# Block transposes on VectorE and four-row-tile scores in a fused attention and MLP kernel

## The chip, the cores and the metric

The kernel runs on one core of a Trainium2 chip. Its metric is device microseconds of the whole program. A profiled execution gives, beside its time, the span from the first to the last instruction and a record of every instruction; the engines are TensorE (PE for matmuls, PEld for the weight loads ahead of them), VectorE (DVE), ScalarE (ACT), GpSimd (POOL, which here mostly issues DMAs) and SyncE (SP, which issues the stores).

## The reference

Sigmoid attention over 8 batches, 12 heads, 448 positions and 64 columns a head; its result, with heads put side by side, is the input of a two-layer MLP with a gated sigmoid.

```
q, k, v: (8, 12, 448, 64)        w_in: (768, 2048)   w_out: (2048, 768)   beta: (2048,)

scores = q @ k.T / sqrt(64) - log(448)
attn   = sigmoid(scores) @ v                          # (8, 12, 448, 64)
x      = attn.transpose(0, 2, 1, 3).reshape(3584, 768)
h      = x @ w_in
out    = (h * sigmoid(beta * h)) @ w_out              # (3584, 768), float32
```

Inputs are float32; the kernel casts them to float16 as they are loaded, accumulates in float32 and stores float32.

## The kernel before

**Units.** A slot is a pair of heads of one batch: six slots a batch, 48 in all. A duo is two slots, four heads. `load_duo` (L82) fetches q, k and v of four heads with DMAs from the POOL queue: partition p of 112 takes the four consecutive positions 4p to 4p+3, 256 values of each head. So column tile s4 of a head holds the positions 4p+s4, and the keys' four tiles and the queries' columns stay in that order through the whole kernel; the stores at the end undo it.

**From raw to scores.** `put_in_order` (L120) copies one slot's q and k on VectorE so that the two heads' 64 columns lie side by side for each s4. `transposes` (L129) turns that into eight transposes on TensorE (128 columns by 112 rows each, written to the PSUM tile `qkT_ps`), and one VectorE copy brings them to `qkT`: rows 0 to 63 are the first head, 64 to 127 the second, columns are positions. `scores` (L141) multiplies a tile of 112 keys with up to 448 queries, contracting 64 rows; the two heads of the slot lie on the two halves of the rows. The result `sco` is two PSUM banks, and one ACT instruction (L162) makes its sigmoid into `attnT`. There are two `sco` tiles. `attend` (L172) multiplies with v: eight matmuls, the two heads on the two halves of the output's partitions, into a PSUM tile of its own (`ps_av`), and a VectorE cast (L188) puts it into the batch's `xT`.

**The dense part.** `dense1` (L194) makes one 128-row piece of h from `xT` (six matmuls, L200), its sigmoid on ACT (L208) and the product on VectorE (L211) into `gt`. `dense2` (L215) makes half of a 128-row output tile (sixteen matmuls, L219), copied by VectorE (L229) into `osb`; after the second half the tile is stored from SP, in up to two pieces that put the rows back to their positions. `dense1`, `dense2` and `transposes` share three PSUM buffers (`ps_one`).

**Order.** Everything is issued in an order written out by hand; each engine runs its own instructions in that order.

- Start: loads of three duos and the first weights; eleven idle matmuls to keep TensorE running; `put_in_order` and `transposes` for the first slots.
- First loop: the six slots of batch 0, queries 0 to 223, each with `attend` of the slot before. Further weights and duos are fetched in between.
- Second loop: the same slots with queries 224 to 447, with eleven dense units filled in; `load_w_out` is fetched here.
- Main loop: steps h = 12 to 95, two to a slot. A step computes two key tiles of a slot's scores (L152, four matmuls), then as many dense units from a list (`filler_stream`) as a time budget allows. At a slot's first step `attend` of the slot before comes first and `put_in_order(s + 2)` is queued; at its second step `transposes(s + 2)` follows the scores. Every second slot the duo three ahead is loaded. The raw tiles have three buffers, the v tiles five.
- End: the last `attend` and the remaining dense units.

Of the kernel before, what the change touches and what calls it, by code (L numbers as in the profile page):

```python
# [14 lines left out]
def kernel(  # L15
# [10 lines left out]

    nc = tc.nc
# [6 lines left out]
    P = 128  # L41
    S4 = 4
    SP = S // S4
    NPAIR = H // 2
    NHC = DM // P
# [7 lines left out]
    NSLOT = B * NPAIR  # L53

# [3 lines left out]
    qkp = ctx.enter_context(tc.tile_pool(name="qkp", bufs=2))  # L58
    qkTp = ctx.enter_context(tc.tile_pool(name="qkTp", bufs=8))
    attnp = ctx.enter_context(tc.tile_pool(name="attnp", bufs=8))  # L60
# [5 lines left out]
    ps_av = ctx.enter_context(tc.tile_pool(name="ps_av", bufs=1, space=bass.MemoryType.PSUM))  # L66
    ps_one = ctx.enter_context(tc.tile_pool(name="ps_one", bufs=3, space=bass.MemoryType.PSUM))

    ident = const.tile([P, P], FP16, name="ident")
# [8 lines left out]

# [3 lines left out]
    def load_duo(d: int, what="qkv", slots=(0, 1)):  # L82
        b, tp = divmod(2 * d, NPAIR)
        if d not in raws:
            raws[d] = rawp.tile([SP, 2, 4, S4 * D], FP16, tag="raw", name="raw")
            vs[d] = vp.tile([SP, 4, S4 * D], FP16, tag="v16", name="v16")
        h0, h1 = 2 * slots[0], 2 * slots[-1] + 2
        for nm, dst, srct in (("q", raws[d][:, 0], q), ("k", raws[d][:, 1], k), ("v", vs[d], v)):
            if nm in what:
                nc.gpsimd.dma_start(  # L90
                    out=dst[:, h0:h1, :],
                    in_=srct[b, 2 * tp + h0 : 2 * tp + h1].rearrange(
                        "h (p s4) d -> p h (s4 d)", s4=S4
                    ),
                )

# [16 lines left out]

# [4 lines left out]
    qks = {}  # L118

    def put_in_order(s: int):  # L120
        d, i = divmod(s, 2)
        qk = qkp.tile([SP, 2, S4, 2, D], FP16, tag="qk", name="qk16")
        nc.vector.tensor_copy(  # L123
            out=qk.rearrange("p r s4 h d -> p r h s4 d"),
            in_=raws[d][:, :, 2 * i : 2 * i + 2, :].rearrange("p r h (s4 d) -> p r h s4 d", s4=S4),
        )
        qks[s] = qk

    def transposes(s: int):  # L129
        qk = qks.pop(s)  # L130
        ps = ps_one.tile([P, 2, S], FP16, tag="one", name="qkT_ps")
        for reg in range(2):
            for s4 in range(S4):
                nc.tensor.transpose(  # L134
                    ps[:, reg, s4 * SP : (s4 + 1) * SP], qk[:, reg, s4], ident[0:SP, 0:SP]
                )
        t = qkTp.tile([P, 2, S], FP16, tag="qkT", name="qkT")
        nc.vector.tensor_copy(out=t, in_=ps)  # L138
        qkT[s] = t

    def scores(s: int, c0: int, n: int, jts):  # L141

        t = qkT[s]
        per = S // n
        todo = []
        for i in range(0, len(jts), per):
            js = jts[i : i + per]
            sco = ps_sc.tile([SP, 2, 512], FP32, tag="sco", name="sco")
            for u, jt in enumerate(js):
                for hh in range(2):  # L150
                    lo, hi = hh * D, (hh + 1) * D
                    nc.tensor.matmul(  # L152
                        sco[:, hh, u * n : (u + 1) * n],
                        t[lo:hi, 1, jt * SP : (jt + 1) * SP],
                        t[lo:hi, 0, c0 : c0 + n],
                        start=True,
                        stop=True,
                    )
            todo.append((js, sco))
        for js, sco in todo:  # L160
            at = attnp.tile([SP, 2, S], FP16, tag="attnT", name="attnT")
            nc.scalar.activation(  # L162
                out=at,
                in_=sco[:, :, 0:S],
                func=AF.Sigmoid,
                bias=nlogs[0:SP, 0:1],
                scale=MSCALE,
            )
            for u, jt in enumerate(js):
                at_tiles[s, jt, c0] = at[:, :, u * n : (u + 1) * n]  # L170

    def attend(s: int, c0: int, n: int):  # L172
        b, tp = divmod(s, NPAIR)
        d, i = divmod(s, 2)
        if b not in xTs:
            xTs[b] = xTp.tile([P, NHC, S], FP16, tag="xT", name="xT")
        av = ps_av.tile([P, 512], FP32, tag="av", name="av_ps")
        for jt in range(S4):
            at = at_tiles.pop((s, jt, c0))
            for hh in range(2):  # L180
                nc.tensor.matmul(  # L181
                    av[hh * D : (hh + 1) * D, 0:n],
                    vs[d][:, 2 * i + hh, jt * D : (jt + 1) * D],
                    at[:, hh],
                    start=(jt == 0),
                    stop=(jt == S4 - 1),
                )
        nc.vector.tensor_copy(out=xTs[b][:, tp, c0 : c0 + n], in_=av[:, 0:n])  # L188

# [25 lines left out]
    def dense2(w: int, t: int, half: int):  # L215
        gt = gts[w]
        m2 = ps_one.tile([P, HALF], FP32, tag="one", name="m2_ps")
        for dc in range(NDC):
            nc.tensor.matmul(  # L219
                m2,  # L220
                gt[:, dc, t * P : (t + 1) * P],
                w_out16[:, dc, half * HALF : (half + 1) * HALF],
                start=(dc == 0),
                stop=(dc == NDC - 1),
            )
        if half == 0:
            osbs[w, t] = outp.tile([P, DM], FP32, tag="osb", name="osb")
        osb = osbs[w, t]
        nc.vector.tensor_copy(out=osb[:, half * HALF : (half + 1) * HALF], in_=m2)  # L229
        if half == 1:  # L230
            c, end = t * P, (t + 1) * P
            while c < end:
                b, s4, p0 = 2 * w + c // S, (c % S) // SP, c % SP
                n = min(end - c, SP - p0)
                rows = out[b * S : (b + 1) * S].rearrange("(p s4) dm -> s4 p dm", s4=S4)
                r0 = c - t * P
                nc.sync.dma_start(out=rows[s4, p0 : p0 + n], in_=osb[r0 : r0 + n, :])
                c += n
            osbs.pop((w, t))
# [6 lines left out]
    def filler_stream():  # L246

        for c0 in (0, QH):
            for dc in range(NDC):
                yield M1H_US, 0, lambda dc=dc, c0=c0: dense1(0, dc, c0, QH)  # L250
        for b in range(B):
            if b > 0:
                for dc in range(NDC):
                    yield M1_US, 2 * NPAIR * (b + 1), lambda b=b, dc=dc: dense1(b, dc)
            for t in tiles_after(b):
                for half in range(2):
                    yield M2_US, 0, lambda b=b, t=t, half=half: dense2(b // 2, t, half)
# [9 lines left out]

    with tc.manual_schedule():
        load_duo(0, "qk", (0,))
        make_identity(nc, ident)  # L270
# [10 lines left out]
        load_duo(0, "qk", (1,))  # L281
        load_duo(0, "v")
        load_duo(1)
        load_duo(2)
        load_w_in(0)
        load_w_in(1)
        put_in_order(0)
        transposes(0)
        put_in_order(1)
        transposes(1)  # L290
        put_in_order(2)


        for s in range(NPAIR):
            scores(s, 0, QH, range(S4))
            if s >= 1:
                attend(s - 1, 0, QH)
            if s + 2 < NPAIR:
                transposes(s + 2)
            if s + 3 < NPAIR:  # L300
                put_in_order(s + 3)
            if s == 0:
                load_w_in(2)
            if s == 1:
                load_duo(3)
            if s == 2:
                load_w_in(3)
            if s == 4:
                load_duo(4)

        for s in range(NPAIR):
            scores(s, QH, QH, range(S4))
# [7 lines left out]
            if s == 4:  # L320
                put_in_order(6)
            if s == 5:
                put_in_order(7)
                transposes(6)
# [7 lines left out]
        for h in range(2 * NPAIR, 2 * NSLOT):  # L332
            s, g = divmod(h, 2)
            if g == 0:
                if s == NPAIR:
                    attend(s - 1, QH, QH)
                else:
                    attend(s - 1, 0, S)
                if s > NPAIR and s + 2 < NSLOT:
                    put_in_order(s + 2)  # L340
                if s % 2 == 0:
                    d = s // 2 + 2 if s == NPAIR else s // 2 + 3
                    while d <= s // 2 + 3 and d < NSLOT // 2:
                        load_duo(d)
                        d += 1
            scores(s, 0, S, (2 * g, 2 * g + 1))
            if s == NPAIR and g == 0:
                transposes(s + 1)
                put_in_order(s + 2)
            if g == 1 and s + 2 < NSLOT:  # L350
                transposes(s + 2)
            i = h - 2 * NPAIR
            budget += first / 7 if i < 7 else second / 5 if i < 12 else rest
            while at_fill[0] < len(fill):
# [4 lines left out]
                fill_units(1)  # L359
        attend(NSLOT - 1, 0, S)  # L360
# [31 lines left out]
```

## Time and profile before

| | us |
|---|---|
| median of three runs (lowest, highest) | 441.91 (441.15, 443.85) |
| span of the profiled execution | 439.7 |
| PE busy | 423.2 |
| ACT busy | 259.5 |
| DVE busy | 186.1 |
| mean granted TensorE clock | 0.984 of full speed |

What lies around the span is therefore about 2.2 us against the median of the runs. A group's line on the page tells its source line, engine, operation, tiles (written, then read), shape, count, busy time and the mean of one in nanoseconds, then how long the engine stood idle before such instructions and who ended that. The lines that touch the change:

| line | what | count | mean ns |
|---|---|---|---|
| L134 | transposes on PE | 384 | 218 |
| L138 | copy of `qkT_ps` on DVE | 48 | 621 |
| L123 | `put_in_order` on DVE | 48 | 418 |
| L152 | scores on PE | 432 | 356 |
| L162 | sigmoid of the scores on ACT | 192 | 1008 |
| L181 | attend on PE | 432 | 347 |
| L188 | cast of the attend result on DVE | 54 | 568 |

A matmul's duration includes its way through the array, and successive ones overlap; what one costs in a stream is read from start to start.

### The profile page before, as it was taken

How to read it: one execution, taken by the hardware profiler on the slowest of the kernel's cores; microseconds unless marked ns; L12 is line 12 of the kernel's file. 1: busy time of each engine (PE TensorE's matmuls, PEld its weight loads, DVE VectorE, ACT ScalarE, POOL GpSimd, SP SyncE). 2: the span in 40 equal slices, each digit the busy share in tenths (PEclk: the TensorE clock that was granted, in tenths of full speed). 3: DMA queues.
4: the chain of work that ended last, by engine and by line, in shares of the span. 5: the costliest groups of instructions: out<-in, count | busy, mean ns of one | idle time of the engine just before them, and what ended most of it. 6: DMA issues, size and time to landing. Idle time of an engine off the chain costs nothing.

```text
span 439.7 us, 7256 instructions
## 1 busy us (share of the span) xinstructions
PE 423.2 (96%) x3019; PEld 227.0 (52%) x3019; DVE 186.1 (42%) x351; ACT 259.5 (59%) x338; POOL 58.9 (13%) x90
## 2 busy tenths in 40 slices
PE   5789989999999999999999999999999999999995
PEld 2566765544555445544555544554455544455563
DVE  2425553355423554245532455326543255325421
ACT  3598984578635686368744678547854487525400
POOL 8433230110110110100101101101100000000000
PEclk9689999999999999999999999999999999999999
DMA  8999995632435604715326514335142110111022
GB/s 95 198 203 205 208 180 92 99 66 36 63 75 97 100 2 62 134 38 64 43 58 123 93 20 63 71 76 89 17 61 60 37 36 1 33 40 36 1 72 72
DMA packets 45264, 34.28 MB, mean 78 GB/s; under 512 B 4272, under 2 KB 41648, under 8 KB 45232
## 3 DMA queue, kind: packets, MB, share of 16 engines
q0 software_dynamic: 38688, 22.81, 38.0%
q1 hardware_dynamic: 6544, 11.02, 8.7%
q8 instruction: 23, 0.38, 0.3%
q14 instruction: 9, 0.07, 0.0%
HBM read 45.62 MB, written 11.01 MB: 129 GB/s over the span
## 4 chain that ended last, share of the span: by engine, by line
PE 85%; DMA 11%; POOL 2%; issue 1%; DVE 0%; ACT 0%; DVEq 0%; POOLq 0%; ACTq 0%
PE m_ps L219 34%; PE m_ps L200 30%; PE sco L152 9%; PE av_ps L181 8%; DMA raw<-in_k_dram 7%; DMA w_in<-in_moe_w_in_dram 5%; PE qkT_ps L134 4%; POOL raw L90 1%; POOL v L90 0%; ACT attnT L162 0%; DVE gt L211 0%; DVE osb L229 0%; ACT sg L208 0%; DVE qk L123 0%; POOL ident masks.py:199 0%
## 5 line engine op out<-in xcount | busy, mean ns | idle before, releaser
L162 ACT ACTIVATE attnT<-sco,nlogs 112x896 f16<-112x896 f32 x192 | 182.8, 1008 | 112.7 <-PE sco L152 112.7
L200 PE MATMUL m_ps<-xT,w_in 128*128 128x448 f16 (+1 forms) x864 | 154.8, 332 | 0.0
L219 PE MATMUL m_ps<-w_out,gt 128*128 128x384 f16 x896 | 153.2, 326 | 0.0
L211 DVE TENSOR_TENSOR gt<-m_ps,sg 128x448 f16<-128x448 f32 (+1 forms) x144 | 81.5, 573 | 96.5 <-ACT sg L208 94.3
L219 PEld LDWEIGHTS <-gt 128*128 128x128 f16 x896 | 84.9, 98 | 60.6 <-issue 7.5
L200 PEld LDWEIGHTS <-w_in 128*128 128x128 f16 x864 | 81.0, 98 | 62.9 <-issue 8.5
L208 ACT ACTIVATE sg<-m_ps,beta_sb 128x448 f32<-128x448 f32 (+1 forms) x144 | 84.0, 601 | 40.0 <-PE m_ps L200 37.8
L229 DVE COPY osb<-m_ps 128x384 f32<-128x384 f32 x56 | 31.2, 558 | 113.7 <-PE m_ps L219 113.7
L152 PE MATMUL sco<-qkT 64*112 64x448 f16 (+1 forms) x432 | 58.8, 356 | 1.9 <-ACT attnT L162 1.4
L90 POOL DMA_DIRECT2D raw<-in_q_dram x25 | 17.7, 707 | 236.1 <-DVE qk L123 212.8
L181 PE MATMUL av_ps<-attnT,v 112*64 112x448 f16 (+1 forms) x432 | 48.1, 347 | 0.0
L152 PEld LDWEIGHTS <-qkT 64*112 64x112 f16 x432 | 20.7, 128 | 33.5 <-issue 32.3
L188 DVE CAST xT<-av_ps 128x448 f16<-128x448 f32 (+1 forms) x54 | 30.7, 568 | 14.6 <-PE av_ps L181 14.5
L134 PE MATMUL qkT_ps<-ident,qk 112*128 112x112 f16 x384 | 28.0, 218 | 8.2 <-DVE qk L123 6.4
L138 DVE COPY qkT<-qkT_ps 128x896 f16<-128x896 f16 x48 | 29.8, 621 | 12.6 <-PE qkT_ps L134 12.4
L134 PEld LDWEIGHTS <-qk 112*128 112x128 f16 x384 | 20.7, 100 | 24.0 <-issue 11.4
L181 PEld LDWEIGHTS <-v 112*64 112x64 f16 x432 | 20.2, 112 | 22.5 <-issue 16.0
L123 DVE COPY qk<-raw 112x1024 f16<-112x1024 f16 x48 | 20.1, 418 | 10.8 <-DMA raw<-in_k_dram 10.8
L90 POOL DMA_DIRECT2D raw<-in_k_dram x25 | 17.6, 705 | 6.9 <-DMA w_out<-in_moe_w_out_dram 3.9
L90 POOL DMA_DIRECT2D v<-in_v_dram x24 | 16.9, 705 | 10.0 <-PE av_ps L181 4.2
L280 PE MATMUL idle_ps<-still 128*128 128x512 f16 x11 | 4.8, 625 | 1.2 <-DVE still L277 1.2
L108 POOL DMA_DIRECT2D w_out<-in_moe_w_out_dram x4 | 3.0, 745 | 4.4 <-DMA w_in<-in_moe_w_in_dram 3.1
(13 smaller groups left out, 7.7 us busy)
## 6 DMA issues: line engine op xcount, KB each, us to landing
v<-in_v_dram POOLq DMA_DIRECT2D x24, 224.0 KB, 6.3
raw<-in_q_dram POOLq DMA_DIRECT2D x23, 224.0 KB, 4.0
raw<-in_k_dram POOLq DMA_DIRECT2D x23, 224.0 KB, 5.6
w_in<-in_moe_w_in_dram POOLq DMA_DIRECT2D x4, 768.0 KB, 15.9
w_out<-in_moe_w_out_dram POOLq DMA_DIRECT2D x4, 768.0 KB, 19.1
out_dram<-osb SPq DMA_DIRECT2D x8, 336.0 KB, 2.8
out_dram<-osb SPq DMA_DIRECT2D x8, 288.0 KB, 2.9
out_dram<-osb SPq DMA_DIRECT2D x8, 240.0 KB, 2.6
```

The source lines that it names most:

```text
L90: nc.gpsimd.dma_start(out=dst[:, h0:h1, :], in_=srct[b, 2 * tp + h0 : 2 * tp + h1].rearrange("h (p s4) d -> p h (s4 d)", s4=S4),)
L134: nc.tensor.transpose(ps[:, reg, s4 * SP : (s4 + 1) * SP], qk[:, reg, s4], ident[0:SP, 0:SP])
L138: nc.vector.tensor_copy(out=t, in_=ps)
L152: nc.tensor.matmul(sco[:, hh, u * n : (u + 1) * n], t[lo:hi, 1, jt * SP : (jt + 1) * SP], t[lo:hi, 0, c0 : c0 + n], start=True, stop=True,)
L162: nc.scalar.activation(out=at, in_=sco[:, :, 0:S], func=AF.Sigmoid, bias=nlogs[0:SP, 0:1], scale=MSCALE,)
L181: nc.tensor.matmul(av[hh * D : (hh + 1) * D, 0:n], vs[d][:, 2 * i + hh, jt * D : (jt + 1) * D], at[:, hh], start=(jt == 0), stop=(jt == S4 ...
L188: nc.vector.tensor_copy(out=xTs[b][:, tp, c0 : c0 + n], in_=av[:, 0:n])
L200: nc.tensor.matmul(m1[:, 0:n], w_in16[:, hc, dc * P : (dc + 1) * P], xTs[b][:, hc, c0 : c0 + n], start=(hc == 0), stop=(hc == NHC - 1),)
L208: nc.scalar.activation(out=sg[:, 0:n], in_=m1[:, 0:n], func=AF.Sigmoid, bias=0.0, scale=beta_sb[:, dc : dc + 1])
L211: nc.vector.tensor_tensor(out=gts[w][:, dc, off : off + n], in0=m1[:, 0:n], in1=sg[:, 0:n], op=ALU.mult)
L219: nc.tensor.matmul(m2, gt[:, dc, t * P : (t + 1) * P], w_out16[:, dc, half * HALF : (half + 1) * HALF], start=(dc == 0), stop=(dc == NDC - 1),
L229: nc.vector.tensor_copy(out=osb[:, half * HALF : (half + 1) * HALF], in_=m2)
```

## The change

A group is now four heads (a quad, `g`, 24 in all), which is what a duo was.

- `load` fetches q and k of a quad with head and position on the partitions: partition 32h + p takes the fourteen consecutive positions 14p to 14p+13 of head h. v is fetched as before. All of quad 0's q and k come in two DMAs; the q and k of quads 1 and 2 are issued ahead of their v.
- `put_in_order` and `transposes` go, with the identity matrix, the `qk` and `qkT_ps` tiles and the copy of `qkT_ps`. `transpose(g, r)` is one VectorE instruction for q and one for k of a quad: it transposes each 32x32 block in place of its partitions, so that `qkT` holds, for head h on rows 32h to 32h+31, the head's 64 columns as two halves `e`, and the positions in their natural order.
- `scores` contracts 32 rows twice (e = 0 and 1, accumulated in PSUM), with the row given as a tile position. Keys are read with a stride of four. In the main loop a step takes one key tile of both slots of a quad (eight matmuls, two `sco` tiles); in the first two loops a call takes one slot, four key tiles, half the queries.
- The main loop counts quads: at jt = 0 both slots of the quad before are attended; `transpose` of the next quad follows the scores of jt = 1 and 2. `ps_av` goes and `ps_one` has four buffers; `attnT` has twelve; `qkT` has four, one per quad.
- An output tile is stored in one piece, in natural order.

```diff
+    def load(g: int, what="qkv"):
+        ...
+                nc.gpsimd.dma_start(
+                    out=raws[g][:, r].rearrange("p b d -> p (b d)"),
+                    in_=srct[b, heads].rearrange("h (p b) d -> (h p) (b d)", b=NB),
+                )
...
-    def put_in_order(s: int):
...
-    def transposes(s: int):
...
+    def transpose(g: int, r: int):
+        if g not in qkT:
+            qkT[g] = qkTp.tile([P, 2, DH, S], FP16, tag="qkT", name="qkT")
+        nc.vector.transpose(
+            out=qkT[g][:, r].rearrange("p e (q b) -> p b e q", b=NB),
+            in_=raws[g][:, r].rearrange("p b (e f) -> p b e f", e=DH),
+        )
+
+    def scores(slots, c0: int, n: int, jts):
...
+            scos = [ps_sc.tile([SP, 2, 512], FP32, tag="sco", name="sco") for _ in slots]
             for u, jt in enumerate(js):
+                for e in range(DH):
+                    for s, sco in zip(slots, scos):
+                        t = qkT[s // 2]
+                        for hh in range(2):
+                            lo = (s % 2 * 2 + hh) * BLK
+                            nc.tensor.matmul(
+                                sco[:, hh, u * n : (u + 1) * n],
+                                t[lo : lo + BLK, 1, e, jt::S4],
+                                t[lo : lo + BLK, 0, e, c0 : c0 + n],
+                                start=(e == 0),
+                                stop=(e == DH - 1),
+                                tile_position=(lo, 0),
+                            )
...
-        av = ps_av.tile([P, 512], FP32, tag="av", name="av_ps")
+        av = ps_one.tile([P, S], FP32, tag="one", name="av_ps")
...
         for s in range(NPAIR):
-            scores(s, 0, QH, range(S4))
+            scores([s], 0, QH, range(S4))
             if s >= 1:
                 attend(s - 1, 0, QH)
-            if s + 2 < NPAIR:
-                transposes(s + 2)
-            if s + 3 < NPAIR:
-                put_in_order(s + 3)
+            if s % 2 == 0 and s // 2 + 1 < QPB:
+                transpose(s // 2 + 1, 0)
+                transpose(s // 2 + 1, 1)
...
         for h in range(2 * NPAIR, 2 * NSLOT):
+            g, jt = divmod(h, S4)
+            if jt == 0:
+                if g == QPB:
+                    attend(NPAIR - 1, QH, QH)
+                else:
+                    attend(2 * g - 2, 0, S)
+                    attend(2 * g - 1, 0, S)
+                for d in (g + 2, g + 3):
+                    if d < NQUAD and d not in raws:
+                        load(d)
+            scores([2 * g, 2 * g + 1], 0, S, [jt])
+            if jt in (1, 2) and g + 1 < NQUAD:
+                transpose(g + 1, jt - 1)
...
+        attend(NSLOT - 2, 0, S)
         attend(NSLOT - 1, 0, S)
```

## The prediction, made before the changed kernel was run

> **What bounds the kernel now.** I read the busy totals first, then three stretches, then the order of weight loads on TensorE (each block of matmuls begins with one, so they show where PE's time goes), then the start.
>
> The page's totals and the table by stretch (columns: length, then busy time and instructions of PE, PEld, DVE, ACT, POOL, then clock, DMA share, GB/s):
>
> ```profile
> PE 423.2 (96%) x3019; PEld 227.0 (52%) x3019; DVE 186.1 (42%) x351; ACT 259.5 (59%) x338; POOL 58.9 (13%) x90
> ...
> 0.00:62.30 62.30, 51.18 (x515) 35.59 (x515) 26.77 (x66) 45.01 (x67) 25.38 (x42) 0.89 1.23 183
> 62.30:395.60 333.30, 333.07 (x2285) 169.65 (x2284) 144.35 (x261) 204.37 (x255) 33.48 (x48) 1.00 0.37 63
> 395.60:439.70 44.10, 38.96 (x225) 21.72 (x222) 15.02 (x25) 10.15 (x16) 0.00 (x0) 1.00 0.16 45
> ```
>
> In the middle 333 us PE is busy throughout at full clock, and every other engine has a third of its time or more free. There, time is saved only by what PE no longer does, in full. The last 44 us are dense work alone, which the change leaves as it is. The first 62 us are not PE's: DMA is saturated.
>
> The middle in close view, weight loads only (start, length, line, shape, count):
>
> ```profile
> 246.07 0.52 PEld L181 LDWEIGHTS <-v 112*64 112x64 f16 x8 [0.32 <-issue]
> 246.94 0.18 PEld L152 LDWEIGHTS <-qkT 64*112 64x112 f16 x4 [0.36 <-issue]
> 247.46 2.01 PEld L200 LDWEIGHTS <-w_in 128*128 128x128 f16 x12 [0.34 <-issue]
> 249.84 0.18 PEld L152 LDWEIGHTS <-qkT 64*112 64x112 f16 x4 [0.37 <-issue]
> 250.35 0.41 PEld L134 LDWEIGHTS <-qk 112*128 112x128 f16 x8 [0.34 <-issue]
> 250.71 0.15 PEld L200 LDWEIGHTS <-w_in 128*128 128x128 f16 x2
> ```
>
> From start to start: an attend (L181) takes 0.87 to 0.88 us, a step of scores (L152) 0.52, a block of eight transposes (L134) 0.36. Twelve dense matmuls (L200) take 2.38; at 0.189 each (448 columns; eighteen of them take 3.41 to 3.51 in the chain of waits) that is 2.27, so entering the scores' tile shape costs 0.11. Four score matmuls at 0.189 would be 0.76; they take 0.52, so the two heads of a pair, on rows 0 to 63 and 64 to 127, run together: 2 x 0.189, plus 0.05 for the first weight load, plus 0.09 of emptying the array. The eight of an attend likewise: 4 x 0.189 + 0.12.
>
> The start, from the chain of waits (start, length, what):
>
> ```profile
> 8.11 8.67 DMA raw<-in_k_dram
> 17.07 19.79 DMA w_in<-in_moe_w_in_dram
> 38.19 20.11 DMA raw<-in_k_dram
> ```
> ```profile
> 58.42 0.43 DVE L123 COPY qk<-raw 112x1024 f16<-112x1024 f16 x1 [2.17 <-DMA raw<-in_k_dram]
> ```
>
> The keys of the sixth load land at 58.30 behind all the weights, and the VectorE queue stands until then.
>
> **The change, part by part.**
>
> *PE loses the transposes.* After 62.3 the trace has 296 transposes, 37 blocks: 37 x 0.36 = 13.3 us, all on the bounding engine. The other 11 blocks lie in the first stretch, where removing them only brings PE sooner to its wait for data.
>
> *Scores.* A step now covers four heads and one key tile: per half e, four matmuls of 32 rows, four row tiles, four PSUM banks; two halves accumulate. Steps stay 96, 78 of them after 62.3. Before, a step was four matmuls in two waves of two; now it is eight in two waves of four, if four tiles run together. Low bound: 0.05 + 2 x 0.189 + 0.09 = 0.52, as before. High bound: only two run at once, as the trace shows, four waves: 0.05 + 4 x 0.189 + 0.09 = 0.90. I take 0.52: the pairs in the trace share the array without any loss (two 0.189 waves account for the step), so the row tiles are independent there. The keys are now read with a stride of four elements by the weight load, and there are eight loads a step. The trace has no strided load. The four loads of a step now span 0.18 at a median of 0.126 each, so they overlap. If the first four came one by one, or each four times as slowly, the step would grow by 3 x 0.047 = 0.14 (112 columns of a load at full rate, 0.047); the second four lie under the first wave's 0.189. I take 0 and keep 0.14 for the range.
>
> The trace shows no four-way packing. The Trainium skill, "TensorE: Matmul & The Clock Gate", section Part 3 (packing small matmuls), measured four row tiles of 32 rows and 512 columns at 3.07 times one after another, not four. By that a wave would be 4 x 0.189 / 3.07 = 0.246, a step 0.114 longer, and the whole 8.9 us longer (430.5); the same section's span model lets them overlap but for 4 ns each, which is the row's picture.
>
> In the first twelve calls, on one pair each, only two tiles are filled: eight waves of 224 columns for four, +0.38 a call on PE. ACT covers this: between 20 and 39 us it works on 1.91 us of sigmoids per call, and PE needs 0.9 of scores and 0.5 of attend. Were that cover gone, it would cost 12 x 0.38 = 4.6.
>
> *Attends.* Two of them now stand together once per four steps. The second enters without a switch: it saves 0.12, and a pair saves another 0.14 of entering from dense work, but then one more score step is entered from dense work, +0.11. Net 0.15 per four-head group, some 19 groups after 62.3: 2.9 us. The av tile moves into the ring of m_ps, which grows from three to four and loses the transposes' tile; a buffer comes round after four units, 4.5 us at the dense rate, against 0.64 (ACT L208) + 0.62 (DVE L211) to empty it. Nothing.
>
> *VectorE.* It loses 48 copies of 418 ns and 48 of 621, 49.9 us, and gains 48 block transposes of 128x896. The trace has none. Low bound: the copy of as many elements, 0.62 us. Nearest row for one element at a time: the cast of av (L188) takes 620 ns for 448 columns and 388 for 224, that is 1.04 ns each and 0.16 fixed, so 896 make 1.09 us. High bound: each scattered two-byte write counts double, 2.0. I take 1.09 (52 us in all). DVE stays near 43%. A transpose stands ahead of the step's gt products, which wait at least 2 us for their dense matmuls and the sigmoid anyway; so up to about 3 us it costs nothing. Without that cover a group would pay 2 x 1.09.
>
> *ACT.* In a dense-in phase a group of four steps is 8 sigmoids of scores (two take 1.91) and about 10 of dense (0.636): 14.0 us. PE's share: 60 x 0.189 + 4 x 0.52 + 3 x 0.11 + 1.78 = 15.5. ACT stays under PE, but at 90%. Both score tiles of a step now finish together, some 0.2 later for the first. The tightest spot is two score steps with only two dense units between: 2.9 us, against 0.69 to ACT's start and 1.91 of work. It fits by 0.1 to 0.3 us when ACT is not behind. I take 0.
>
> The skill speaks against the change here: "TensorEngine Tiling (Array Packing)", section PSUM Bottleneck, warns that emptying PSUM may bind once the matmuls are packed. The trace has that work at 14.0 against 15.5, so by rule and by row the sum stays; only jitter is at stake.
>
> *DMA and queues.* Queries and keys are fetched in runs of 14 rows per partition instead of 4; same bytes. The fetches on POOL keep a depth of eight and the weights stand at the same byte of the stream, so the sixth group's keys can't land much before 58; I take 57 (q one microsecond earlier). The blocked point moves: before, the copy for slot 10 stood in the VectorE queue ahead of the products of step 16; now transpose(5, 0) stands ahead of those of step 17. Behind it wait three gt products, then PE for a PSUM buffer. PE arrives sooner: the third slot's scores no longer wait for transposes (14.7 instead of 18.1, as slot 1 shares slot 0's load), and four blocks and 1.3 us of their waits are gone. If q lands at 56.8, the transpose ends at 57.9, the products at 59, and step 19's scores begin at about 59.7; before they began at 64.63, with one attend (0.88) more done. Gain 4.0; 2 if the landing stays at 58.3, 7 if it does not bind. PE stands about 3 us before that; the clock row of the page fell to 6 tenths in the slice from 11 to 22 us, after a wait of 5, and as much again would cost 2 us at most: the lower gain holds it. Output rows are now stored in one piece per tile, on SP, behind the same copy: nothing on the path.
>
> *Sum.* 439.7 - 13.3 - 2.9 - 4.0 = 419.5 of span. The median of the runs, 441.9, lies 2.2 above the span, so 421.7.
>
> **Rivals.**
>
> 1. *The row tiles run two at a time.* +0.38 x 78 = 29.6: 451, slower. For: nothing in the trace runs four wide; all four write the same PSUM partitions, in four banks. Against: the two-wide rows show no loss at all. It decides from +0.26 us a step (20.2/78).
> 2. *Weight loads show.* +0.14 x 78 = 10.9: 432.6. For: a stride of four and twice the loads. Against: loads overlap in the trace.
> 3. *VectorE transposes are slow.* DVE per group in a dense-in phase is 10 x 0.62 + 2 x 0.62 + 2T; with T = 4 it equals PE's 15.5. At T = 5 the eleven such groups (112 dense units, ten to a group) lose 1.9 us each: 443. For: a scattered two-byte write. Against: 1.04 ns an element in the trace.
> 4. *The start binds less than I think.* If transfers in longer runs land 2 to 3 us sooner and the attends' gain is full, 416 to 418.
>
> **How the numbers follow.** My case (416 to 427): 0.63. Rival 2 and partial forms of it, with ACT's jitter (427 to 437): 0.18. Rival 4 below 416: 0.07. Rivals 1 and 3: 0.08. Between: 0.04. The range, 415 to 433, takes in my case, rival 2 and most of rival 4. About 1% can be told from no change here. Faster by over 1% (under 437.5): 0.87; within 1%: 0.05; slower: 0.08.
>
> **What would show it.** Right: no PE block between scores and dense work; score steps of 0.52 from load to next block; four score matmuls starting within some 10 ns; PE full from about 58 us on; DVE transposes near 1.1 us. Wrong: steps of 0.66 (loads) or 0.90 (two-wide); PE idle behind sco with ACT late; DVE waits longer than 3 us; a gap on PE after 60 us.

## The result, and the profile after

The changed kernel takes 466.21 us (465.99 to 467.1), the kernel before 441.73: a ratio of 1.0557, 95% interval 1.0531 to 1.0582. It is slower by 5.6%, where 4.6% faster was forecast. The profiled execution has a span of 464.2 us, 44.7 more than the forecast's sum.

The page of the changed kernel: totals, the line shares of the chain that ended last, and the groups of the scores and the new transposes (engine, operation, tiles, shape, count, then busy time, mean ns, idle time ahead).

```profile
PE 422.7 (91%) x3067; PEld 229.6 (49%) x3067; DVE 319.8 (69%) x303; ACT 260.9 (56%) x338; POOL 49.4 (11%) x86
...
PE m_ps L201 30%; DVE qkT L117 27%; PE m_ps L182 14%; PE av_ps L164 9%; PE sco L134 9%; DVE gt L193 6%; ACT sg L190 1%; DMA raw<-in_q_dram 1%; DVE osb L211 1%; ACT attnT L145 0%; DVE xT L171 0%; POOLq L339 0%
...
L117 DVE STREAM_TRANSPOSE qkT<-raw 128x896 f16<-128x896 f16 x48 | 193.6, 4061 | 4.1 <-DMA raw<-in_q_dram 4.1
...
L134 PE MATMUL sco<-qkT 32*112 32x448 f16 (+1 forms) x864 | 74.0, 390 | 20.2 <-DVE qkT L117 19.8
```

A transpose takes 4.06 us, not 1.09. They stand on 27% of the chain, and DVE is busy for 320 us instead of 186. Split at the beginning of step 19 of the main loop (64.63 us before, 89.50 after; columns as in the table by stretch above):

```profile
0.00:89.50 89.50, 61.76 (x563) 43.96 (x564) 59.05 (x56) 49.18 (x71) 21.00 (x38) 0.96 0.82 133
89.50:464.20 374.70, 360.90 (x2505) 185.68 (x2504) 260.73 (x248) 211.73 (x267) 28.41 (x48) 1.00 0.29 60
```

From step 19 to the end it takes 374.7 us, as the kernel before does (375.1): what PE saves there without its transposes is lost again to waits. So the loss, 24.9 us, lies ahead of step 19. (The 0.96 of clock in the first line is too high: this trace has no clock record before 44.6 us, and its score calls of 1.68 us up to 42 us are those that e2, below, shows at a granted clock of 0.50.) The chain there (start, length, what):

```profile
5.26 15.55 DVE qkT L117 x4
...
23.93 7.77 DVE qkT L117 x2
...
53.70 3.96 DVE qkT L117
...
58.77 3.92 DVE qkT L117
```

Four transposes stand one after another from 5 us on and two more from 24 us, and the next scores wait for the last of them each time. In the main loop the same length does its harm in another way:

```profile
169.66 4.06 DVE L117 STREAM_TRANSPOSE qkT<-raw 128x896 f16<-128x896 f16 x1
...
172.66 1.06 PEld L182 LDWEIGHTS <-w_in 128*128 128x128 f16 x7 [0.28 <-issue]
173.36 2.56 DVE L193 TENSOR_TENSOR gt<-m_ps,sg 128x448 f16<-128x448 f32 x4
...
174.23 2.43 PE L182 MATMUL m_ps<-xT,w_in 128*128 128x448 f16 x12 [0.25 <-DVE gt L193]
```

The products that empty the PSUM buffers are queued behind the transpose until 173.36; by then four dense units have filled the ring, and PE, which needs a matmul every 0.189 us, loads its next weights only at 174.23.

### The profile page after: what moved, and what is told of

The parts are those of the page before. It is cut to its first block, busy times and chain, and to the rows that moved or that the text cites. A ratio compares the mean times of both kernels' runs of the same rounds, so it can differ in the third digit from the quotient of the medians.

```text
span 464.2 us, 7204 instructions
## 1 busy us (share of the span) xinstructions
PE 422.7 (91%) x3067; PEld 229.6 (49%) x3067; DVE 319.8 (69%) x303; ACT 260.9 (56%) x338; POOL 49.4 (11%) x86
## 4 chain that ended last, share of the span: by engine, by line
PE 61%; DVE 33%; issue 2%; ACT 2%; DMA 1%; POOLq 0%
PE m_ps L201 30%; DVE qkT L117 27%; PE m_ps L182 14%; PE av_ps L164 9%; PE sco L134 9%; DVE gt L193 6%; ACT sg L190 1%; DMA raw<-in_q_dram 1%; DVE osb L211 1%; ACT attnT L145 0%; DVE xT L171 0%; POOLq L339 0%
## 5 line engine op out<-in xcount | busy, mean ns | idle before, releaser
L117 DVE STREAM_TRANSPOSE qkT<-raw 128x896 f16<-128x896 f16 x48 | 193.6, 4061 | 4.1 <-DMA raw<-in_q_dram 4.1
L182 PE MATMUL m_ps<-xT,w_in 128*128 128x448 f16 (+1 forms) x864 | 159.8, 337 | 11.1 <-DVE gt L193 11.1
L134 PE MATMUL sco<-qkT 32*112 32x448 f16 (+1 forms) x864 | 74.0, 390 | 20.2 <-DVE qkT L117 19.8
L211 DVE COPY osb<-m_ps 128x384 f32<-128x384 f32 x56 | 34.5, 617 | 70.2 <-PE m_ps L201 70.2
L134 PEld LDWEIGHTS <-qkT 32*112 32x112 f16 x864 | 39.2, 187 | 53.1 <-issue 29.9
L164 PE MATMUL av_ps<-attnT,v 112*64 112x448 f16 (+1 forms) x432 | 45.4, 352 | 2.0 <-DVE xT L171 1.8
L83 POOL DMA_DIRECT2D raw<-in_q_dram x24 | 13.1, 544 | 279.4 <-DVE qkT L117 227.8
L164 PEld LDWEIGHTS <-v 112*64 112x64 f16 x432 | 23.0, 116 | 20.9 <-issue 8.9
L88 POOL DMA_DIRECT2D v<-in_v_dram x24 | 17.5, 730 | 12.0 <-PE av_ps L164 10.1
L83 POOL DMA_DIRECT2D raw<-in_k_dram x24 | 13.0, 542 | 0.3 <-DMA raw<-in_q_dram 0.3
L96 POOL DMA_DIRECT2D w_in<-in_moe_w_in_dram x4 | 3.4, 846 | 0.5 <-DMA raw<-in_k_dram 0.3
```

The source lines that it names most:

```text
L83: nc.gpsimd.dma_start(out=raws[g][:, r].rearrange("p b d -> p (b d)"), in_=srct[b, heads].rearrange("h (p b) d -> (h p) (b d)", b=NB),)
L88: nc.gpsimd.dma_start(out=vs[g], in_=v[b, heads].rearrange("h (p s4) d -> p h (s4 d)", s4=S4))
L117: nc.vector.transpose(out=qkT[g][:, r].rearrange("p e (q b) -> p b e q", b=NB), in_=raws[g][:, r].rearrange("p b (e f) -> p b e f", e=DH),)
L134: nc.tensor.matmul(sco[:, hh, u * n : (u + 1) * n], t[lo : lo + BLK, 1, e, jt::S4], t[lo : lo + BLK, 0, e, c0 : c0 + n], start=(e == 0), s ...
L164: nc.tensor.matmul(av[hh * D : (hh + 1) * D, 0:n], vs[g][:, 2 * i + hh, jt * D : (jt + 1) * D], at[:, hh], start=(jt == 0), stop=(jt == S4 ...
L182: nc.tensor.matmul(m1[:, 0:n], w_in16[:, hc, dc * P : (dc + 1) * P], xTs[b][:, hc, c0 : c0 + n], start=(hc == 0), stop=(hc == NHC - 1),)
```

## The experiments

One table first. "Step" is a score step from its first weight load to the next block (median after step 19); "step 19" is when that step begins; all from the traces in us. The times are medians, e14's a single run. A probe of time alone may leave out the order of positions: e2, and e4, e7, e8, e13 and e14, which build on it, e3, and e11 for its first four quads do not put each query and key back to its position, so they do not compute the reference's result. The changed kernel, e1, e5, e6, e9, e10, e12 and e15 do.

| kernel | transpose | step | step 19 at | from there to the end | time |
|---|---|---|---|---|---|
| before | none | 0.52 | 64.6 | 375.1 | 441.7 |
| changed | 4.06 | 0.574 | 89.5 | 374.7 | 466.2 |
| e2 contiguous output | 1.10 | 0.574 | 64.3 | 362.3 | 428.4 |
| e3 changed, near keys | 4.06 | 0.52 | 93.3 | 372.3 | 466.1 |
| e4 e2 + quads in the start | 1.10 | 0.574 | 65.4 | 362.3 | 429.3 |
| e5 pairs as four bytes | 0.94 | 0.70 | 69.6 | 372.0 | 443.3 |
| e6 changed, in pieces | 1.10 to 1.38 each | 0.574 | 87.5 | 362.3 | 450.3 |
| e7 e2 + near keys | 1.10 | 0.52 | 65.9 | 358.3 | 425.4 |
| e8 e2 + two idle matmuls | 1.10 | 0.574 | 71.5 | 362.3 | 435.0 |
| e9 contiguous + copy | 1.10 + 0.94 | 0.574 | 68.8 | 362.3 | 434.1 |
| e10 e9 + two idle matmuls | 1.10 + 0.94 | 0.574 | 75.8 | 362.3 | 439.2 |
| e11 contiguous for four quads | 1.10, then 4.06 | 0.574 | 71.5 | 374.7 | 447.4 |
| e12 blocks kept in order | 1.10 (q), 0.97 + 0.27 (k) | 0.49 to 0.51 | 65.5 | 358.1 | 423.2 |
| e13 e4 + two idle matmuls | 1.10 | 0.574 | 64.8 | 362.3 | 428.6 |
| e14 e2 + six idle matmuls | 1.10 | 0.574 | 63.9 | 362.3 | 428.0 |
| e15 e12 + start of e13 | as e12 | 0.49 to 0.51 | 62.8 | 358.1 | 422.7 |

**What makes the transpose slow.**

```diff
+        nc.vector.transpose(out=runs_of_896, in_=f16)       # and 448, and 64
+        for st in (2, 4, 8, 14, 16):
+            nc.vector.transpose(out=dst_with_step_st, in_=f16[:, 0])
+        nc.vector.transpose(out=l32_runs, in_=f32)           # and with a step of 14
+        nc.vector.tensor_copy(out=scattered_as_in_L117, in_=f16)
```

> The changed kernel, with eleven more VectorE instructions after its last dense unit: the block transpose of 128x896 with its output in one contiguous run, of half as many elements, of 64 elements with runs and with output steps of 2, 4, 8, 14 and 16 elements, of 448 pairs taken as four-byte elements (runs, and steps of 14), and a plain copy with the same scattered output. Only the durations of these are read. Theory A, the scattered write costs: 896 elements in runs take 1.1 us, the short ones grow with the step, the copy with the scattered output is slow too (about 4 us). Theory B, the block transpose of two-byte elements costs 4.4 ns an element whatever its output: runs take 4.06, the short ones are all alike, the scattered copy takes about 1.1. The four-byte form takes about half of the two-byte form of its kind by either.

Groups of that kernel's DVE, at its end:

```profile
L348 DVE COPY pad<-raw 128x896 f16<-128x896 f16 x1 | 2.1, 2085 | 0.0
L344 DVE STREAM_TRANSPOSE pad<-raw 128x64 f16<-128x64 f16 x5 | 1.9, 386 | 0.2
...
L332 DVE STREAM_TRANSPOSE pad<-raw 128x896 f16<-128x896 f16 x1 | 1.1, 1102 | 0.0
L347 DVE STREAM_TRANSPOSE pad<-raw 128x448 f32<-128x448 f32 x1 | 0.9, 939 | 0.0
L335 DVE STREAM_TRANSPOSE pad<-raw 128x448 f16<-128x448 f16 x1 | 0.6, 645 | 0.0
L346 DVE STREAM_TRANSPOSE pad<-raw 128x448 f32<-128x448 f32 x1 | 0.6, 645 | 0.0
L339 DVE STREAM_TRANSPOSE pad<-raw 128x64 f16<-128x64 f16 x1 | 0.2, 245 | 0.0
```

The five short ones as one line of the trace (count: min, median and max ns):

```profile
L344 DVE STREAM_TRANSPOSE pad<-raw x5: 252/445/461, 462.6 to 464.2; 128x64 f16<-128x64 f16 x5
```

Theory A holds. The same 896 elements in runs take 1102 ns: (1102 - 645) / 448 = 1.02 ns an element and 0.19 us fixed. The five short ones, one by one in the trace, take 252, 320, 461, 453 and 445 ns for output steps of 2, 4, 8, 14 and 16 elements against 245 in a run: no cost at 4 bytes, some at 8, and from 16 bytes on a constant (453 - 245) / 64 = 3.3 ns more for each element. Four-byte elements suffer far less (939 against 645 for 448), and a plain copy also pays, though less: 2085, half of the 4 us that theory A had put on it. The four-byte forms are not half of the two-byte ones either, as was expected by both theories: 645 against 1102 in runs, 939 against 4061 scattered.

The Trainium skill, "VectorE: DVE Perf Modes", section The three transpose paths, gives 311 ns for a block transpose of 128x128. By e1's rows 64 elements at 245 and 1.02 more for each of another 64 would make 310, an estimate; but e12, below, has that size, with output in runs of 32 elements, and takes 268 to 271. So the page's figure is near what output in runs costs; the section says nothing of a step.

```diff
-            out=qkT[g][:, r].rearrange("p e (q b) -> p b e q", b=NB),
+            out=qkT[g][:, r].rearrange("p e (b q) -> p b e q", b=NB),
```

> The changed kernel with the transposes' output in contiguous runs (block after block) instead of steps of 14 elements; scores read the same addresses, so positions are permuted in them. Theory A (scattered write): L117 falls from 4.06 to about 1.1 us and the time to 424 to 430 (the forecast of 421.7 and 4 for score steps of 0.57 instead of 0.52). Theory B (the transpose itself): L117 stays at 4.06 and the time at 466.

428.4 us, ratio to before 0.9719 (0.9684 to 0.9754). The order of two indices in the output's layout is worth 37.8 us.

```profile
L117 DVE STREAM_TRANSPOSE qkT<-raw 128x896 f16<-128x896 f16 x48 | 52.8, 1101 | 4.6 <-DMA raw<-in_q_dram 4.5
```

**Where the 37.8 us lie.** Two kernels cut them in two.

```diff
-            if jt in (1, 2) and g + 1 < NQUAD:
-                transpose(g + 1, jt - 1)
+            if g + 1 < NQUAD:
+                cut = (0, 4, 8, 11, 14)                      # blocks
+                transpose(g + 1, 0, cut[jt], cut[jt + 1])
+                transpose(g + 1, 1, cut[jt], cut[jt + 1])
```

> The changed kernel, its scattered transposes cut in four pieces each, a piece for q and one for k after the scores of each of the four steps; DVE's total stays at 320 us, but no piece is over 1.4 us. Theory 1, the 4 us pieces hurt by blocking what is queued behind them on DVE: PE's waits in the main loop (some 11 us) go, the start stays: 453 to 457. Theory 2, DVE's total per group in the dense-in phases (15.6 us against 15.7 of PE) is what binds: 464 to 468.

```diff
+        if g < 4:
+            cols = qkT[g][:, r].rearrange("p e (b q) -> p b e q", b=NB)
```

> The changed kernel with contiguous output in the transposes of the first four quads alone (positions of these are permuted in their scores), the others scattered as they are. Theory: the loss against contiguous transposes throughout is 22 us before step 19 and 16 us of blocking in the main loop; the first goes: 442 to 446. Rival: time gained at the start is waited for later (data not there, or DVE behind): above 455.

In pieces, 450.3: the part after step 19 falls to 362.3, exactly that of contiguous transposes, though DVE works longer still (330.7 us against 319.8). These are its pieces:

```profile
L117 DVE STREAM_TRANSPOSE qkT<-raw 128x256 f16<-128x256 f16 x80 | 95.8, 1377 | 0.0
L117 DVE STREAM_TRANSPOSE qkT<-raw 128x192 f16<-128x192 f16 x80 | 73.6, 1100 | 0.0
```

Waits of the matmuls from step 19 on in the changed kernel (us in all, times, longest); in pieces there is none:

```profile
PE m_ps L182 <- DVE gt L193: 6.5, 7, 1.8
PE m_ps L201 <- DVE gt L193: 3.1, 7, 1.2
PE av_ps L164 <- DVE gt L193: 0.2, 1, 0.2
```

So in the main loop it was never DVE's total (theory 2) but one instruction of 4 us standing in the queue. With contiguous output in the first four quads alone, 447.4: the start falls by 18 us (step 19 at 71.5), and what follows stays at 374.7. It missed the 442 to 446 that I expected by 1.4, because quads 4 and 5, still scattered, are transposed ahead of step 19 too. By the traces, 12.4 us are blocking from step 19 on (374.7 against e2's 362.3) and 25.2 lie ahead of it (89.5 against 64.3): 18.0 of them with the first four quads, 7.2 with the four transposes of quads 4 and 5.

**The score steps.**

```diff
-                                t[lo : lo + BLK, 1, e, jt::S4],
+                                t[lo : lo + BLK, 1, e, jt * SP : (jt + 1) * SP],
```

> The changed kernel with 112 neighbouring key columns in each weight load instead of every fourth one (so a tile holds other keys than its values). Theory: the stride makes the loads slow, which shows once per step; the steps fall from 0.57 to 0.52 and the time by 3 to 5 us, to 461 to 463. Rival: it is the four-tile shape, the step stays at 0.57 and the time at 466.

> The kernel with contiguous transposes (428.4), with 112 neighbouring key columns in each weight load (a tile holds other keys than its values). Where PE binds, the 0.05 us per step must show: 84 x 0.053 = 4.4 us less, 424.0. Rival, as in the kernel with slow transposes: no change, 428.

Weight loads of the changed kernel and of e3 (count: min, median and max ns):

```profile
L134 PEld LDWEIGHTS <-qkT x864: 172/194/213, 13.2 to 411.1; 32*112 32x112 f16 x173
```
```profile
L134 PEld LDWEIGHTS <-qkT x864: 121/124/214, 13.3 to 412.5; 32*112 32x112 f16 x173
```

The stride is the cause: the step falls from 0.574 to 0.52, the figure of two-wide packing before. So four row tiles do run four wide without loss; their four matmuls start within 10 ns of each other in the trace. On the slow kernel the median does not move (466.1; runs from 464.6 to 467.5): its trace gains 2.4 us after step 19, but begins step 19 3.8 us later, and why it does so is not shown. On e2 near keys are worth 3.0 in the medians and 4.0 after step 19. I expected 461 to 463 of the first, and was wrong in the way the second expectation names as its rival.

```diff
+        src = raws[g][:, r].rearrange("p b d -> p (b d)").bitcast(FP32)
+        dst = qkT[g][:, r].rearrange("p s e -> p (s e)").bitcast(FP32)
+        nc.vector.transpose(out=dst.rearrange("p (q b) -> p b q", b=NB), in_=...)
...
-                                t[lo : lo + BLK, 1, e, jt::S4],
+                                t[lo : lo + BLK, 1, jt::S4, e],
```

> The changed kernel with the transposes done on pairs of neighbouring columns as four-byte elements (14 blocks instead of 28, steps of 14 pairs in the output); the two halves of the contraction are then the even and the odd columns, queries are read with a step of two elements and keys with a step of eight. Theory (the scattered two-byte write made the cost): L117 takes 0.94 us and the time falls to 424 to 432, as with contiguous output, the steps being 0.57 to 0.65 us. Rival: reads with steps slow the matmuls (a wave of 0.378 instead of 0.189): steps near 0.95 and 458 us.

443.3, ratio 1.0039 (1.0017 to 1.006), where 424 to 432 was expected. The transposes take 0.94 as expected, but a load with a step of eight elements takes about 0.18 before its matmul can stream (0.08 with four, 0.05 with one, from load to second load in the trace), so the steps grow to 0.70. Of the 14.9 us between this and e2, 9.6 come after step 19, and 77 x 0.126 = 9.7 is what the longer steps make there: what the four-byte elements save on DVE is lost on PE's weight loads.

**The start.** Contiguous transposes reach step 19 at 64.3, where 59.7 was forecast. In e2's trace:

```profile
12.00:28.00 16.00, 16.00 (x151) 11.96 (x148) 4.66 (x9) 11.79 (x13) 4.06 (x7) 0.50 1.25 204
```

PE works for all of 16 us at a granted clock of 0.50: a call of the first loop (the `scores` and the `attend` of one slot) takes 2.57 us (1.68 of scores, 0.89 of attend), not the 1.9 of ACT.

```diff
-            scores([s], 0, QH, range(S4))
+            scores([2 * g, 2 * g + 1], 0, QH, (2 * i, 2 * i + 1))     # e4, e13
...
+            for _ in range(2):                                        # e8, e13; 6 in e14
+                nc.tensor.matmul(warm, still[:, 0:P], still, start=True, stop=True)
```

> The kernel with contiguous transposes (428.4), and in the first two loops scores for both slots of a quad at once, two key tiles per call, so that all four row tiles are filled there too; attends follow one call later. Theory: a stream of score matmuls on two of four row tiles, with attends between, leaves the granted clock at 0.50 (12 to 28 us there, PE busy throughout); filling the array brings the clock to 1 and halves the score matmuls: calls every 1.9 us (ACT) instead of 2.57, 4 to 6 us less in all, 422 to 425. Rival: the clock stays at 0.50 until dense matmuls come; the score part alone gets shorter, and the calls every 1.9 to 2.0 us are ACT's; 424 to 426, with 0.50 in the clock's column.

> The kernel with contiguous transposes (428.4), with idle matmuls of 128x512 on zeros in the first loop, four after the first call and two after each other. Theory: matmuls on all 128 rows and columns lift the granted clock, which stood at 0.50 from 12 to 28 us; calls then come every 1.9 to 2.0 us instead of 2.57 and the main loop is reached 3 to 5 us sooner: 423.5 to 426. Rival: the clock is not lifted by so few of them; each costs 0.43 us at half clock and the time grows by 3 to 5 us, to 432 to 433.

> The kernel with contiguous transposes and both slots of a quad per call in the first two loops (429.3), with two idle matmuls of 128x512 after each call of the first loop, where PE waits for ACT anyway (0.8 us a call). Theory, the clock answers to how much of the array is at work: with the idle matmuls rows times time come to some 0.85 of the array instead of 0.55, the clock rises to 1 before 20 us, calls come every 1.95 us instead of 2.83: 423 to 426. Rival, only long dense blocks lift it: the clock stays 0.50 to 28 us and the time at 429 to 431.

> The kernel with contiguous transposes and six idle matmuls after each call of the first loop instead of two. Theory, occupied share of the array: two left it at 0.73 and the clock at 0.50; six bring 0.81, and the clock should rise within two calls, before 20 us; the time is 430 to 436 since each call then takes 2.8 us. Rival, only dense matmuls on real data lift the clock: 0.50 throughout the first loop, calls of 5.1 us, 442 or more.

Filled tiles alone (e4, 429.3) leave the clock at 0.50 and make the calls 2.83 us long: a call fills both score tiles together, so the next one waits for ACT. Two idle matmuls a call (e8, 435.0) only cost; six (e14, one run) give 428.0. With the tiles filled, two a call (e13) raise the clock as its theory said, but the time is 428.6 and not 423 to 426. The times of e4 and e8 lie above both of their forecasts, that of e14 below its two.

The same window of e8, e13 and e14 (the clock is the third number from the end):

```profile
12.00:28.00 16.00, 16.00 (x118) 9.05 (x116) 3.97 (x7) 8.19 (x9) 4.12 (x6) 0.50 1.25 204
```
```profile
12.00:28.00 16.00, 13.48 (x146) 7.32 (x144) 3.85 (x7) 10.92 (x12) 4.12 (x6) 0.71 1.25 203
```
```profile
12.00:28.00 16.00, 15.52 (x168) 9.69 (x167) 3.98 (x8) 10.90 (x12) 4.11 (x6) 1.00 1.25 202
```

The record of e14's clock is borne out by its matmuls: the idle ones at the very beginning start 0.427 us apart, those in the first loop 0.216.

How much of the array is at work can be estimated from the traces: 448 columns take 0.189 us at full clock and twice that at half, and a matmul fills as many of the 128 rows and 128 columns of the array as its operands have. The granted clock holds for 3.41 us or a multiple of it, so I take stretches of that length, end to end from the first clock record on. In e2 those from 10 to 27 us have shares of 0.44 to 0.52, and the clock stays at half; the next, with the first dense matmuls, has 0.82, and the clock rises. In e8 those from 10 to 37 us have 0.50 to 0.73 and leave it at half; one of 0.77 raises it. In e13 a stretch of 0.74 raises it at 17.5 us, in the kernel before one of 0.73 at 19.4 us. The time in which columns stream at all does not sort them: it is 92% in e8's stretch of 0.73 and 95% in one of e7 with 0.71, which do not raise the clock, and 84% and 83% in those of e13 and of the kernel before, which do. So the clock follows how much of the array works, not how long PE is busy. Zeros count: the first rise, 3.9 to 6.7 us into the traces whose clock record reaches so far back, has nothing but idle matmuls before it. The boundary for a rise, about 0.73, is an estimate; by it one rise in the kernel before, at 29.7 us behind 0.69, is an exception. A clock that is full is kept at less: e13 loses it behind a stretch of 0.32, e8 behind 0.36, while e14, which has it from 6.7 us on, is never under 0.39 up to 70 us and does not lose it.

The Trainium skill, "TensorE: Matmul & The Clock Gate", Part 1, says that a busy window of some 3.4 us releases the full clock. In e2, 16 us of PE at 0.50, busy by the profile's count, contradict that as it stands.

In time the clock gave little: e14 begins step 19 at 63.9, e13 at 64.8, against 64.3. The idle matmuls fill the time that they win, and in the second loop at full clock a call of e2 takes 2.77 us of PE (1.01 of scores, 0.51 of attend, 1.25 of dense work) against 2.28 to 2.46 in the kernel before. Why step 19 does not come before 62.8 in any kernel is not fully settled.

**Versions that use this.**

```diff
+        nc.vector.transpose(out=blk, in_=...)                 # contiguous, scratch
+        nc.vector.tensor_copy(
+            out=qkT[g][:, r].rearrange("p e (q b) -> p e q b", b=NB),
+            in_=blk.rearrange("p b e q -> p e q b"),
+        )
```

> The changed kernel with each block transpose written in contiguous runs into a scratch tile, and a VectorE copy behind it that brings the positions into their natural order (reads with a step of 64 elements, writes in runs of 14). Theory: reads with a step cost nothing, the copy takes about 1.1 us, pieces of 2.2 us do not block the main loop; two more microseconds before the first scores: 429 to 432. Rival: scattered reads cost as scattered writes do (copy of 2 to 4 us): 445 or more.

> Both of the last two edits: 425 to 429 if the idle matmuls lift the clock, and 1 to 3 us above the kernel with the copy where they do not.

e9: 434.1, ratio 0.984 (0.9808 to 0.9871), above the 429 to 432 expected. A copy that reads with a step and writes in runs takes 0.94 us, less than half of the one that scatters its writes:

```profile
L123 DVE COPY qkT<-blk 128x896 f16<-128x896 f16 x48 | 45.2, 941 | 1.7
```

Step 19 comes 4.5 us later than in e2, more than the two expected, at a clock that stays low longer (to 33.2 us against 30.5). With the idle matmuls (e10) 439.2, as e8 had shown them to cost without lifting the clock; that is 5.1 above e9 where 1 to 3 was expected.

```diff
+        if r == 0: nc.vector.transpose(out=dst_in_block_order, in_=src)
+        else:      nc.vector.transpose(out=dst[:, 0:3], in_=src[:, 0:12] as (c u))  # keys, by tile
+                   nc.vector.transpose(out=dst[:, 3, 0:2], in_=src[:, 12:14])
...
+            for c in range(0, NB, S4):                        # v, four pieces
+                nc.gpsimd.dma_start(out=vs[g][lo : lo + BLK, :, 0 : n * D], in_=...)
...
+                nc.sync.dma_start(out=rows[r % S // BLK], in_=osb[r0 : r0 + BLK, :])
```

> A version that keeps every element in its place with contiguous transposes: queries stay in block order and the stores put the rows back, key blocks are written so that each key tile is one contiguous run (tiles of 128, 128, 96 and 96 keys), v is loaded in four pieces to match. Theory: as the kernel with contiguous transposes and neighbouring keys (425.4), with 0 to 3 us for three more v pieces per quad on POOL and 112 instead of 28 stores: 424 to 429. Rival: the smaller v pieces hold up the start (POOL spends 0.5 to 0.7 us on each): 430 to 436.

> The version that keeps every element in its place, with the first two loops of the run before last (both slots per call, two idle matmuls). 420 to 425 if the clock rises; otherwise 1 to 3 us above that version alone.

e12: 423.2, ratio 0.9601 (0.9574 to 0.9629); e15: 422.7, ratio 0.9584 (0.956 to 0.9607). Both beat the kernel before and the changed one, and lie within 1.5 us of where the forecast had put the change itself; from each other they cannot be told. The smaller pieces of v do not hold up the start (step 19 at 65.5).

## Why the prediction was wrong

1. *The VectorE term failed.* I took 1.09 us for a transpose and 2.0 as its high bound; 4.06 was measured. 1.09 is right for output in runs (1.10). The bound rested on "each scattered two-byte write counts double", which no row of the trace supported; the trace had no scattered write at all, and e1 puts it at about four times (1.02 + 3.3 ns an element). A bound that is itself a guess closed the range at 433.
2. *"Up to about 3 us it costs nothing"* was not refuted, but it did not help, as the real length lay beyond it. Two pieces of 2.2 to 2.8 us together in a step cost nothing (e6); single ones of 4.06 cost 12.4 us after step 19. I named what stands behind the transpose, but the sum was made at 1.09 only.
3. *Rival 3 named the mechanism and mispriced it.* It compared DVE's total with PE's per group, a tie at 4 us. At 4.06 the kernel lost 44.5 us against the forecast: not by the total, but by blocking (12.4) and ahead of step 19 (25.2), where scores wait for the transposes themselves. That second place was not in the rival. The remaining 7 us are the later start and the longer steps of points 5 and 6, which e2 has too, less 1.5 that PE's part won.
4. *PE's part was right.* No transpose block stands between scores and dense work; four tiles run together; e2 needs 362.3 us after step 19 where before needs 375.1 + 0.88 for the attend already done there. The 13.6 saved, with 77 x 0.053 = 4.1 given to longer steps, make 17.7 against 16.2 forecast for the part after 62 us; e7, whose steps are not longer, saves 17.6 by itself. The 1.4 to 1.5 more than forecast are not assigned.
5. *The strided loads* I took at 0, with 0.14 as the bound: 0.053, some 4 us. The 3.07 for four row tiles of the Trainium skill, "TensorE: Matmul & The Clock Gate", Part 3, did not come true here: a step of 0.52 with near keys is two waves at full rate.
6. *The start* was 4.6 us later than forecast even in e2. I had put it down to the landing of the sixth load; DVE waits for data 4.5 us in all, nearly all of it for the very first load. The cover "ACT works 1.9 us a call" needed PE at full clock, and PE stood at half: six calls of 2.57 instead of 1.9 would make 4.0 us, an estimate that no run confirms, as e13 and e14 spend on idle matmuls what the clock wins.
7. *ACT's 90%* held after step 19, where no score step of e2 but step 19 itself is over 0.6 and no matmul waits for another engine. Ahead of it the "I take 0" for the tightest spot failed: steps 13, 14, 15, 17 and 18 of e2 take 0.80 to 0.98 instead of 0.574, 1.7 us in all, because the second score tile waits for ACT's sigmoid of the step before (which ends at 49.20 in step 14, whose second tile begins at 49.25). How the 4.6 us of point 6 divide between this and the clock stays open.

## What to carry to other kernels

Look at the output's step of a VectorE instruction before its element count: two-byte elements written 16 bytes or more apart cost about four times what a run costs, in a transpose, and reading with a step is the cheaper side. An instruction that is harmless by its engine's total can still stop the bounding engine through the queue behind it; cut it in pieces, and see above all whether it stands at the start, where nothing covers it. Where the trace has no row for an operation, its high bound has to come from a neighbour that is worse than it, or the range must say that it has none.

## What the runs showed of the hardware that I had not expected

- Block transposes of two-byte elements on VectorE: 1.02 ns an element with output in runs or 4 bytes apart (64 elements in 245 and 252 ns), 320 ns at 8 bytes, 445 to 461 from 16 bytes on. Four-byte elements 56 bytes apart: 939 ns for 448, against 645 in runs.
- Weight loads on TensorE of 112 two-byte columns: 0.05 us for neighbours, 0.08 every fourth, 0.18 every eighth.
- A TensorE that is busy without a pause (16.00 of 16.00 us in e2) can stay at half clock when about half of its array is at work (0.44 to 0.52, an estimate); stretches of 3.41 us with 0.74 and more raised the clock in these traces, and idle matmuls on zeros count towards it.
